# Local attention between two long convolutions: group norms on GpSimd, a flat count of background pieces, predicated first keys, earlier spectra

## The chip, the cores and the metric

The kernel runs on one NeuronCore of a Trainium2 chip. The metric is device time of one launch in microseconds (us), lower is better. The core's engines run side by side and meet through semaphores: TensorE (PE; its weight loads are listed as PEld), VectorE (DVE), ScalarE (ACT), GpSimd (POOL), and the queue on SyncE (SP) that issues most DMA transfers.

## The reference, cut to what matters

The data are `x` of 2048 tokens by 512 channels in bf16. Four residual layers follow each other, A, B, A, B:

```python
x = A_u
x = x + A(layernorm(x))   # long convolution per channel, by FFT, + u * Dskip
x = x + B(layernorm(x))   # local attention
x = x + A(layernorm(x))   # the same kernel spectra again
x = x + B(layernorm(x))   # the same weights again

def B(x):                 # 32 heads of 16; window 8, dilation 2
    q, k, v = split(x @ wqkv)                       # 512 -> 3 * 512
    idx = pos[:, None] - 2 * arange(8)[None, :]     # 8 keys behind each query, 2 apart
    attn = softmax(where(idx >= 0, q . k[idx] * 16 ** -0.5, -1e9))
    return (attn . v[idx]) @ wo
```

As the dilation is 2, even and odd tokens never meet: attention splits into two parities of 1024 tokens.

## The kernel before

**Stages.** Up to about 258 us the convolution kernels are built and the first convolution runs; the change leaves this part alone, but for the size of one statistics tile. `b_layer` is called twice (258 to 374 us and 438 to 557.5 us of the profiled span), `a_layer` once between them (374 to 438 us). In these functions the order of work on PE, DVE and ACT is the order in which it is written (`manual_schedule`); GpSimd and SP also take their instructions in program order, and an instruction that waits holds up what is queued behind it on its engine.

**`b_layer`, its steps.** The loop at the end runs 36 steps t = 0 to 35 (`N = 4 * NB`, `NB` = 9). A step handles 2 token blocks of one of four job sets n = t // 9. Set n has parity `n // 2` and one half of the heads (`n % 2`). A step consists of:

- `logits(t)`: 16 small products (L1098) into the one 4-bank PSUM tile S, then the exponential on ACT (L1101) that writes PT and so frees S;
- `work`: background pieces in the order of their due times. `proj` (L1056, two pieces of two matmuls 128x512) makes 512 tokens of one q or k feature group; DVE takes the result to a tile `st` (L1061), and SP sends even and odd features of it to `KS` or `QS` (L1072), where even and odd heads lie apart. `vproj` (L1081, one piece) makes V for one block, `out` (L1152, two pieces) the output projection of 128 tokens. All have PSUM tiles `psG`, of which there are three. The number of pieces of a step follows from the due times;
- `values(t - 2)`: 16 products of PT with V into the one PSUM tile O (L1117), then reciprocal and product on DVE (L1121, L1125);
- every third step `turn_o`: an SP transpose of the result (`oS`) and a GpSimd copy into `oT` (L1134);
- `late(t)`: the layer norm of token groups 2 and 3 (see below).

**`sets`** holds two pairs `KS`, `QS`, used by turns: logits(9) is the first step that reads those of n = 1. Their `proj` jobs run in steps 4 to 8.

**Groups.** The tokens are cut into four groups of four slots of 128; groups 0 and 1 are parity 0, groups 2 and 3 parity 1. Groups 0 and 1 are normed and transposed ahead of the loop. For groups 2 and 3 `late` does it in the loop: `gather` (bn_stats on DVE, L212), `aggregate` (DVE, L223, then a root on GpSimd, L225 and L226), `scales` (DVE, L230, L231), four `norm` calls (DVE, L260) into `xq`, two SP transposes into `xt` (L1216), and four GpSimd copies from `xt` into `XU` (L1220, its view here is `xnT`). The `proj` and `vproj` jobs of n = 2 and 3 read these columns; their earliest step is t = 13, that of the `out` jobs t = 24. For group 2, `late` gathers at t = 2 and 3, aggregates at 4, scales and norms at 6, and norms and transposes at 7; for group 3 all of it comes three steps later.

**First keys.** Ahead of the loop four `proj` jobs of n = 0 run: k = 0 and 2 (q and k of the first 512 tokens), then 1 and 3 (the next 512). Of k = 0 and 2, the first 240 columns (`FIRST`) go from PSUM to `QS` and `KS` by predicated copies on DVE (L1069), the others by ACT and SP DMAs. The loop starts behind all four.

**The tail.** The last steps emit `values` of two steps, `ahead` (dummy matmuls on L1284 and half an output piece), and `turn_last`, which transposes on PE in place of the DMA.

**`a_layer`** takes 16 chunks. For chunk k: `s1` (forward transform, evacuated into Z), `turns` (SP transposes of Z into zt, two chunks each) or `turn_pe`, `s2` (spectrum, L882, evacuated to `xc` on ACT, L886), `product` (DVE, L894, L895 and two more), `inverse` (into VT) and `final` (into X). At i = 14 and 15 it also gathers the statistics of groups 0 and 1 for the next layer, four slots of 384 columns at a time.

Of the kernel before, what the change touches and what calls it, by code (L numbers as in the profile page):

```python
# [11 lines left out]
ALU = mybir.AluOpType  # L12
# [87 lines left out]
def slot(m):  # L100

    g, i = m // 4, m % 4
    return 8 * (g % 2) + 2 * i + g // 2
# [93 lines left out]
class LnStats:  # L197
# [58 lines left out]
        nc.vector.scalar_tensor_tensor(self.nb[:, js], self.sums[:, 0, js], -1.0 / D, self.rstd[:, js], ALU.mult,  # L256
                                       ALU.mult)

    def norm(self, dst, src, j):
        self.nc.vector.tensor_scalar(dst, src, self.rstd[:, j:j + 1], self.nb[:, j:j + 1], ALU.mult, ALU.add)  # L260


def turn(nc, zt, Z, g0, n):
# [553 lines left out]
def a_layer(nc, tc, C, X, kt_dram, XU, ln_b, finish):  # L817

    with ExitStack() as es:
# [119 lines left out]
        with tc.manual_schedule(engines={mybir.EngineType.PE, mybir.EngineType.DVE, mybir.EngineType.Activation}):  # L939
            s1(0, on_dve)  # L940
            finish()
            s1(1, on_act)
            s1(2, on_dve)
            s1(3, on_act)
            zpair(0)
            warm(2)
            turn_pe(0)
            s1(4)
            s2(0, True)
            turns(2)  # L950
            turn_pe(1)
            s1(5, on_dve)
            for i in range(16):
                if i > 0:
                    s2(i)
                product(i)
                if i > 0:
                    inverse(i - 1, i > 10)
                if i + 6 < 16:
                    s1(i + 6)  # L960
                    if i % 4 == 1:
                        turns(i + 3)
                        turns(i + 5)
                if i >= 5:
                    final(i - 5, on_dve if i in (6, 8) else on_act)
                if i in (14, 15):
                    ln_b.gather(X, 0, (i - 14) * 4, (i - 14) * 4 + 4)
            final(11)
            inverse(15)
            for k in range(12, 16):  # L970
                final(k)


def b_layer(nc, tc, C, X, Wt, ln_b, XU, store=None, ln_next=None):

    with ExitStack() as es:
# [67 lines left out]
        st = {}  # L1044
        on_act, on_dve = nc.scalar.copy, nc.vector.tensor_copy

        def proj(n, k, eng=on_dve, early=False):

            par, fp = n // 2, n % 2
            f2, which, h = k // 4, k // 2 % 2, k % 2  # L1050
            if h == 0:
                st[n, which] = stp.tile([128, 1024], BF, name="st", tag="st")
            f0 = which * 512 + (fp * 2 + f2) * 128
            ps = gps([128, 512])
            for ct in range(4):
                nc.tensor.matmul(ps[:], wqk[:, ct, f0:f0 + 128], xnT[:, ct, par, UF + h * 512:UF + h * 512 + 512],  # L1056
                                 start=(ct == 0), stop=(ct == 3))
                if ct == 1:
                    yield
            if not early:  # L1060
                eng(st[n, which][:, h * 512:h * 512 + 512], ps[:])  # L1061
            else:
                eng(st[n, which][:, FIRST:512], ps[:, FIRST:512])
            if h or n == 0:
                T = sets[n % 2][1 - which]
                x0 = 0 if n else FIRST if early else 512 * h
                if early:
                    for e in range(2):
                        nc.vector.copy_predicated(T[:, e, f2, UF:UF + FIRST], par_rows[:, e:e + 1].to_broadcast([128, FIRST]),  # L1069
                                                  ps[:, 0:FIRST])  # L1070
# [35 lines left out]
        def values(t):  # L1106
            par, fp = t // NB // 2, t // NB % 2
            pt = PT[t % 3]
            for x in range(2):
                assert (par, fp, (t % NB * 2 + x) % NB) in ready, (t, x, done)  # L1110
            O = psO.tile([128, 16, DH + 1], F32, name="O", tag="O")
            for i in range(4):
                for sl in range(4):
                    x, e = sl // 2, sl % 2
# [74 lines left out]

        with tc.manual_schedule(engines={mybir.EngineType.PE, mybir.EngineType.DVE, mybir.EngineType.Activation}):  # L1190
            def warm(n):
                O = psO.tile([128, 16, DH + 1], F32, name="O", tag="O")
                for _ in range(n):
                    nc.tensor.matmul(O[:].rearrange("p a b -> p (a b)"), ident[:],
                                     C["F1"][:, 0:2].rearrange("p j r k -> p (j r k)")[:, 0:272], start=True, stop=True,
                                     skip_group_check=True)
            xq = {}

            def late(t):
                for g in (2, 3):  # L1200
                    u, m0 = t - 3 * g + 2, g * 4
                    if u in (-2, -1):
                        for p in range(len(ln_b.parts)):
                            ln_b.gather(X, p, m0 + 2 * u + 4, m0 + 2 * u + 6)
                    elif u == 0:
                        ln_b.aggregate(m0, m0 + 4, C["half"])
                    elif u == 2:
                        ln_b.scales(m0, m0 + 4)
                        xq[g] = ld.tile([128, 4, D], BF, name="xq", tag="xq")
                    if u in (2, 3):  # L1210
                        for i in (2 * u - 4, 2 * u - 3):
                            ln_b.norm(xq[g][:, i], X[:, slot(m0 + i), :], m0 + i)
                    if u == 3:
                        xt = ld.tile([128, 16, 128], BF, name="xt", tag="xt")
                        for h in range(2):
                            nc.sync.dma_start_transpose(xt[:, 8 * h:8 * h + 8],  # L1216
# [28 lines left out]
            fan(0, pt0, 1)  # L1245
            fan(1, pt1, 1)
            warm(6)
            for k in (0, 2):
                for _ in proj(0, k, on_act, True):
                    pass  # L1250
            for k, eng in ((1, on_act), (3, on_dve)):
                for _ in proj(0, k, eng):
                    pass
            psS = banks("b_psS", 1)
            jobs = []
            for n in range(4):
                p = n // 2
                for i, k in enumerate((4, 6, 5, 7) if n == 0 else range(8)):
                    k0 = i + 4 if n == 0 else i
                    jobs.append((NB * n - 1.5 + (k0 // 4 * 4 if n else 4 + i // 2 * 2), 2, proj(n, k), 0 if n < 2 else 13))  # L1260
                jobs += [(NB * n + b // 2 + 1 + b / 100, 1, vproj(p, n % 2, b), 0 if n < 2 else 13) for b in range(NB)]
            jobs += [(N - 9 + .8 * m, 2, out(m), 24) for m in range(8)]
            jobs.sort(key=lambda j: j[0])
# [21 lines left out]
                                     stop=True, skip_group_check=True)  # L1285
                omm(tail[m], m, (0, 1))
            for t in range(N):
                end = done + max(min(total - done, -(-(c - done) // max(1, int(d) - t + 1))) for d, c in due)
                logits(t)
                square()  # L1290
                work(end - 1, t)
                if 2 <= t < N - 1:
                    values(t - 2)
                work(end, t)
                if t >= N - 2:
                    assert not jobs
# [54 lines left out]
def kernel(  # L1351
# [70 lines left out]
```

## Time and profile before

| what | value |
|---|---|
| median of 5 runs (lowest, highest) | 558.1 us (557.04, 559.28) |
| the profiled execution: its own time, its span | 559.23 us, 557.5 us |
| granted TensorE clock, mean | 0.92 |
| busy time over the span: PE, DVE, ACT, POOL | 401.0, 434.1, 355.7, 72.9 us |
| layer B, first (258 to 374 us): PE, DVE, ACT, POOL busy | 101.81, 80.69, 84.62, 31.68 us |
| second convolution (374 to 438 us) | 52.67, 50.94, 47.48, 3.61 us |
| layer B, second (438 to 557.5 us) | 102.47, 77.98, 76.73, 18.27 us |

The span runs from the first to the last instruction of the profiled execution; 1.73 us of its time lie around it. A row of the page's groups gives a line, engine, operation and tile, busy time and mean duration, and the idle time just ahead of it with what ended that. A row of the timeline gives start, duration, engine, line, operation, output and inputs, and in brackets the idle time before it and its releaser. All times are of one execution.

### The profile page before, as it was taken

What the parts mean: (1) busy time and instruction counts of PE and PEld (TensorE: products, weight loads), DVE (VectorE), ACT (ScalarE), POOL (GpSimd) and SP (SyncE); (2) the same over time, 40 slices, a digit from 0 to 9 for tenths busy, and PEclk for the clock granted to TensorE, in tenths of its full rate; (3) what the DMA queues carried; (4) which work ended last, traced back from release to release, by engine and by line L of the source; (5) the groups of instructions that cost most, each with busy time, mean ns of one, the idle gap of its engine ahead of it and who ended that gap; (6) DMA issues with size and microseconds to landing.
All of it is one profiled execution on the core that took longest, in us unless ns stands there. A gap on an engine that the chain in (4) does not pass through costs nothing.

```text
span 557.5 us, 15293 instructions
## 1 busy us (share of the span) xinstructions
PE 401.0 (72%) x6530; PEld 255.9 (46%) x6530; DVE 434.1 (78%) x959; ACT 355.7 (64%) x439; POOL 72.9 (13%) x121
## 2 busy tenths in 40 slices
PE   1200665485668459698995999887898699599987
PEld 0100433354337136465553466555665455346654
DVE  5999998989979997676696576576897869657653
ACT  4999654364536346356766479865888676647762
POOL 0000000000000020543016111250000201611110
PEclk9999998698779778799998799997999999879999
DMA  8201057532463567334236132215782013513452
GB/s 275 111 1 38 2 113 98 86 125 59 95 115 115 116 73 207 65 125 155 93 92 124 54 105 60 39 45 146 165 167 48 2 49 95 121 54 105 100 74 77
DMA packets 100536, 52.79 MB, mean 95 GB/s; under 512 B 85363, under 2 KB 93428, under 8 KB 99188
## 3 DMA queue, kind: packets, MB, share of 16 engines
q1 hardware_dynamic: 97956, 48.01, 37.0%
q0 software_dynamic: 928, 3.41, 1.9%
q8 instruction: 51, 0.84, 0.7%
q10 hardware_dynamic: 1584, 0.39, 0.3%
q14 instruction: 17, 0.14, 0.1%
HBM read 17.96 MB, written 8.13 MB: 47 GB/s over the span
## 4 chain that ended last, share of the span: by engine, by line
PE 32%; DVE 28%; ACT 8%; DMA 6%; issue 4%; SPq 2%; POOL 1%; DVEq 0%; ACTq 0%; POOLq 0%
PE psG L1056 7%; DMA zt<-Z 4%; PE psG L1081 4%; PE O L1117 3%; ACT PT L1101 3%; PE S L1098 3%; DVE Ytab L656 3%; DVE ln_st_b L212 2%; DVE Y2tab L658 2%; PE psG L1152 2%; DVE ta L619 2%; DVE tb L620 2%; DVE st L1061 2%; DVE xq L260 2%; POOL XU L1220 1%
## 5 line engine op out<-in xcount | busy, mean ns | idle before, releaser
L1101 ACT ACTIVATE PT<-S 128x1824 bf16<-128x1824 f32 x72 | 121.7, 1690 | 55.3 <-PE S L1098 55.2
L1056 PE MATMUL psG<-XU,wqk 128*128 128x512 bf16 x256 | 71.8, 397 | 9.0 <-POOL XU L1220 8.3
L1061 DVE CAST st<-psG 128x512 bf16<-128x512 f32 x58 | 39.1, 680 | 27.2 <-PE psG L1056 26.9
L1117 PEld LDWEIGHTS <-PT 128*128 128x128 bf16 x1152 | 38.5, 97 | 21.7 <-DVE on L1125 10.3
L1117 PE MATMUL O<-V,PT 128*128 128x17 bf16 x1152 | 40.3, 171 | 8.1 <-DVE on L1125 7.9
L1081 PE MATMUL psG<-wv,XU 128*128 128x256 bf16 x288 | 39.5, 273 | 1.2 <-DVE st L1061 1.2
L307 PE MATMUL psA<-X,sb_F 128*128 128x128 bf16 x128 | 13.7, 242 | 36.4 <-ACT X L720 35.2
L307 PEld LDWEIGHTS <-sb_F 128*128 128x128 bf16 x256 | 16.9, 105 | 44.2 <-issue 41.8
L1121 DVE RECIPROCAL rd<-O 128x16 f32<-128x16 f32 x72 | 18.2, 253 | 22.7 <-PE O L1117 21.0
L1056 PEld LDWEIGHTS <-wqk 128*128 128x128 bf16 x256 | 21.0, 98 | 29.7 <-issue 14.5
L294 ACT CAST Z<-psA 128x1024 bf16<-128x1024 f32 (+1 forms) x32 | 28.8, 982 | 7.8 <-PE psA L307 7.8
L675 PE MATMUL psk<-Ytab,Xtab 128*32 128x64 bf16 x1024 | 24.2, 209 | 12.5 <-issue 6.5
L1125 DVE TENSOR_TENSOR on<-O,rd 128x256 bf16<-128x256 f32 x72 | 30.5, 424 | 2.5
L678 PE MATMUL psk<-Y2tab,Xtab 128*32 128x48 bf16 x1024 | 23.4, 206 | 12.1 <-issue 10.0
L1098 PEld LDWEIGHTS <-KS 32*128 32x128 bf16 x1152 | 19.0, 95 | 28.1 <-issue 25.4
L1098 PE MATMUL S<-QS,KS 32*128 32x114 bf16 x1152 | 28.6, 216 | 4.5 <-ACT PT L1101 2.7
L656 DVE TENSOR_TENSOR Ytab<-Ytab,MA 128x2048 bf16<-128x2048 bf16 (+1 forms) x33 | 30.6, 927 | 0.2
L658 DVE TENSOR_TENSOR Y2tab<-Ytab,MB 128x2048 bf16<-128x2048 bf16 (+1 forms) x33 | 30.5, 925 | 0.0
L684 ACT CAST KTq<-psk 128x1024 bf16<-128x1024 f32 (+1 forms) x9 | 8.3, 918 | 34.3 <-issue 28.9
L332 PE MATMUL psA<-zt,sb_C 128*128 128x512 bf16 x30 | 14.9, 524 | 20.7 <-DMA zt<-Z 20.7
L678 PEld LDWEIGHTS <-Xtab 128*32 128x32 bf16 x1024 | 21.2, 103 | 16.6 <-issue 15.7
L1081 PEld LDWEIGHTS <-XU 128*128 128x128 bf16 x288 | 24.9, 98 | 6.8 <-issue 1.3
(245 smaller groups left out, 1050.1 us busy)
## 6 DMA issues: line engine op xcount, KB each, us to landing
kt_scratch<-Kt SPq DMA_DIRECT2D x4, 1024.0 KB, 3.9
Kt<-kt_scratch SPq DMA_DIRECT2D x4, 1024.0 KB, 6.2
QS<-st SPq DMA_DIRECT2D x24, 128.0 KB, 2.0
KS<-st SPq DMA_DIRECT2D x24, 128.0 KB, 3.2
X<-in_A_u_dram SPq DMA_DIRECT2D x4, 512.0 KB, 5.2
out_dram<-X SPq DMA_DIRECT2D x16, 128.0 KB, 1.7
k_scratch<-KTq SPq DMA_DIRECT2D x7, 256.0 KB, 2.2
KT<-k_scratch SPq DMA_DIRECT2D x7, 256.0 KB, 2.9
```

The lines of the kernel that those rows point to most:

```text
L294: self.nc.scalar.copy(dst, src)
L307: nc.tensor.matmul(o, F1[:, j, r, :], rhs_j(j), start=True, stop=not dk)
L656: nc.vector.tensor_tensor(v(Y[:, :, :, q * EYB:(q + 1) * EYB, :]), src, vm(self.mult(self.MA, lev, hc, EYB)), ALU.mult)
L658: nc.vector.tensor_tensor(v(Y2[:, :, :, (q - 1) * EYB:q * EYB, :]), src, vm(self.mult(self.MB, lev, hc, EYB)), ALU.mult)
L678: nc.tensor.matmul(psk[32 * g:32 * g + 32, ds, EYB:], xs, Y2[:, 1 - m // 2, h, :, t], start=False, stop=(m == 3), skip_group_check=True)
L1056: nc.tensor.matmul(ps[:], wqk[:, ct, f0:f0 + 128], xnT[:, ct, par, UF + h * 512:UF + h * 512 + 512], start=(ct == 0), stop=(ct == 3))
L1061: eng(st[n, which][:, h * 512:h * 512 + 512], ps[:])
L1081: nc.tensor.matmul(ps[:].rearrange("p h d -> p (h d)"), xnT[:, ct, par, NQ * b + 1:NQ * b + 1 + NK], wv[:, ct, fp * 256:fp * 256 + 256], s ...
L1098: nc.tensor.matmul(S[:, i, sl * NQ:(sl + 1) * NQ], KS[r, e, f2, b * NQ + 1:b * NQ + 1 + NK], QS[r, e, f2, UF + b * NQ:UF + b * NQ + NQ], s ...
L1101: nc.scalar.activation(pt[:, 0:16 * NQ].rearrange("k (i x) -> k i x", i=4), S[:, :, 0:4 * NQ], ACT.Exp, scale=DH ** -0.5)
L1117: nc.tensor.matmul(O[:, x * 8 + i * 2 + e, :], pt[:, c0:c0 + 128], V[:, par * NB + b, (fp * 2 + f2) * 8 + i * 2 + e, :], start=True, stop= ...
L1125: nc.vector.tensor_tensor(on.rearrange("q (h d) -> q h d", d=DH), O[:, :, 0:DH], rd[:].unsqueeze(2).to_broadcast([128, 16, DH]), ALU.mult)
```

## The change

1. `norm` takes an engine, and `late` norms groups 2 and 3 on GpSimd: gathers at t = 0 and 1, aggregate at 2, scales, norms, transposes and copies all at 3; for group 3 two steps later.
2. The pieces of a step: four for t < 4 and from t = 28 on, three between, more only where the due times ask for it. Due times of the `proj` jobs are one step earlier, and those of n = 0 lie closer together.
3. `begun`, `placed` and `spread` stand for the first four `proj` jobs: q and k of the first 512 tokens go to `QS` and `KS` by predicated copies alone, in two parts of which the second stands behind logits(0); the product of k = 3 also comes behind logits(0) and uses the PSUM tile O.
4. At t = 33 to 35 the order of `values`, `ahead` and `turn_last` is another.
5. In `a_layer`, `s2` runs one chunk further ahead from i = 6 on, `s1(5)` stands behind the first product, the last finals stand behind the last inverses, and the gathers of groups 0 and 1 are spread over i = 10 to 15. For that, the statistics of layer 2 have three parts of 256, 128 and 128 columns in place of two of 384 and 128.

```diff
--- before.py
+++ after.py
@@ -256,8 +256,8 @@
         nc.vector.scalar_tensor_tensor(self.nb[:, js], self.sums[:, 0, js], -1.0 / D, self.rstd[:, js], ALU.mult,
                                        ALU.mult)
 
-    def norm(self, dst, src, j):
-        self.nc.vector.tensor_scalar(dst, src, self.rstd[:, j:j + 1], self.nb[:, j:j + 1], ALU.mult, ALU.add)
+    def norm(self, dst, src, j, eng=None):
+        (eng or self.nc.vector).tensor_scalar(dst, src, self.rstd[:, j:j + 1], self.nb[:, j:j + 1], ALU.mult, ALU.add)
 
 
 def turn(nc, zt, Z, g0, n):
@@ -949,13 +949,19 @@
             s2(0, True)
             turns(2)
             turn_pe(1)
-            s1(5, on_dve)
             for i in range(16):
-                if i > 0:
+                if 0 < i < 7:
                     s2(i)
+                if 6 <= i < 15:
+                    s2(i + 1)
                 product(i)
-                if i > 0:
+                if i == 15:
+                    inverse(14, True)
+                    inverse(15)
+                if 0 < i < 15:
                     inverse(i - 1, i > 10)
+                if i == 0:
+                    s1(5, on_dve)
                 if i + 6 < 16:
                     s1(i + 6)
                     if i % 4 == 1:
@@ -963,11 +969,11 @@
                         turns(i + 5)
                 if i >= 5:
                     final(i - 5, on_dve if i in (6, 8) else on_act)
-                if i in (14, 15):
-                    ln_b.gather(X, 0, (i - 14) * 4, (i - 14) * 4 + 4)
-            final(11)
-            inverse(15)
-            for k in range(12, 16):
+                if 10 <= i < 14:
+                    ln_b.gather(X, 0, 2 * i - 20, 2 * i - 18)
+                if i >= 14:
+                    ln_b.gather(X, 1, 4 * i - 56, 4 * i - 52)
+            for k in range(11, 16):
                 final(k)
 
 
@@ -1044,7 +1050,28 @@
         st = {}
         on_act, on_dve = nc.scalar.copy, nc.vector.tensor_copy
 
-        def proj(n, k, eng=on_dve, early=False):
+        def begun(k, pool=None):
+            f2, which, h = k // 4, k // 2 % 2, k % 2
+            f0 = which * 512 + f2 * 128
+            ps = pool.tile([128, 512], F32, name="O", tag="O") if pool else gps([128, 512])
+            for ct in range(4):
+                nc.tensor.matmul(ps[:], wqk[:, ct, f0:f0 + 128], xnT[:, ct, 0, UF + h * 512:UF + h * 512 + 512],
+                                 start=(ct == 0), stop=(ct == 3))
+            return ps
+
+        def placed(k, ps, a, b):
+            T = sets[0][1 - k // 2 % 2]
+            for e in range(2):
+                nc.vector.copy_predicated(T[:, e, k // 4, UF + a:UF + b], par_rows[:, e:e + 1].to_broadcast([128, b - a]),
+                                          ps[:, a:b])
+
+        def spread(k, ps, eng):
+            T, t = sets[0][1 - k // 2 % 2], stp.tile([128, 1024], BF, name="st", tag="st")
+            eng(t[:, 0:512], ps[:])
+            for e in range(2):
+                nc.sync.dma_start(T[e::2, e, k // 4, UF + 512:UF + 1024], t[e::2, 0:512])
+
+        def proj(n, k, eng=on_dve):
 
             par, fp = n // 2, n % 2
             f2, which, h = k // 4, k // 2 % 2, k % 2
@@ -1057,17 +1084,10 @@
                                  start=(ct == 0), stop=(ct == 3))
                 if ct == 1:
                     yield
-            if not early:
-                eng(st[n, which][:, h * 512:h * 512 + 512], ps[:])
-            else:
-                eng(st[n, which][:, FIRST:512], ps[:, FIRST:512])
+            eng(st[n, which][:, h * 512:h * 512 + 512], ps[:])
             if h or n == 0:
                 T = sets[n % 2][1 - which]
-                x0 = 0 if n else FIRST if early else 512 * h
-                if early:
-                    for e in range(2):
-                        nc.vector.copy_predicated(T[:, e, f2, UF:UF + FIRST], par_rows[:, e:e + 1].to_broadcast([128, FIRST]),
-                                                  ps[:, 0:FIRST])
+                x0 = 0 if n else 512 * h
                 for e in range(2):
                     nc.sync.dma_start(T[e::2, e, f2, UF + x0:UF + h * 512 + 512], st[n, which][e::2, x0:h * 512 + 512])
 
...
@@ -1189,28 +1209,26 @@
 
...
             xq = {}
 
             def late(t):
                 for g in (2, 3):
-                    u, m0 = t - 3 * g + 2, g * 4
-                    if u in (-2, -1):
+                    u, m0 = t - 2 * g + 4, g * 4
+                    if u in (0, 1):
                         for p in range(len(ln_b.parts)):
-                            ln_b.gather(X, p, m0 + 2 * u + 4, m0 + 2 * u + 6)
-                    elif u == 0:
+                            ln_b.gather(X, p, m0 + 2 * u, m0 + 2 * u + 2)
+                    elif u == 2:
                         ln_b.aggregate(m0, m0 + 4, C["half"])
-                    elif u == 2:
+                    elif u == 3:
                         ln_b.scales(m0, m0 + 4)
                         xq[g] = ld.tile([128, 4, D], BF, name="xq", tag="xq")
-                    if u in (2, 3):
-                        for i in (2 * u - 4, 2 * u - 3):
-                            ln_b.norm(xq[g][:, i], X[:, slot(m0 + i), :], m0 + i)
-                    if u == 3:
+                        for i in range(4):
+                            ln_b.norm(xq[g][:, i], X[:, slot(m0 + i), :], m0 + i, nc.gpsimd)
                         xt = ld.tile([128, 16, 128], BF, name="xt", tag="xt")
                         for h in range(2):
                             nc.sync.dma_start_transpose(xt[:, 8 * h:8 * h + 8],
@@ -1245,19 +1263,22 @@
             fan(0, pt0, 1)
             fan(1, pt1, 1)
             warm(6)
-            for k in (0, 2):
-                for _ in proj(0, k, on_act, True):
-                    pass
-            for k, eng in ((1, on_act), (3, on_dve)):
-                for _ in proj(0, k, eng):
-                    pass
+            half = [begun(0), begun(2), begun(1)]
+            for k in range(2):
+                placed(2 * k, half[k], 0, FIRST)
+            spread(1, half[2], on_act)
             psS = banks("b_psS", 1)
+            logits(0)
+            odd = begun(3, psO)
+            placed(0, half[0], FIRST, 512)
+            spread(3, odd, on_dve)
+            placed(2, half[1], FIRST, 512)
             jobs = []
             for n in range(4):
                 p = n // 2
                 for i, k in enumerate((4, 6, 5, 7) if n == 0 else range(8)):
                     k0 = i + 4 if n == 0 else i
-                    jobs.append((NB * n - 1.5 + (k0 // 4 * 4 if n else 4 + i // 2 * 2), 2, proj(n, k), 0 if n < 2 else 13))
+                    jobs.append((NB * n - 2.5 + (k0 // 4 * 4 if n else 4 + i // 2), 2, proj(n, k), 0 if n < 2 else 13))
                 jobs += [(NB * n + b // 2 + 1 + b / 100, 1, vproj(p, n % 2, b), 0 if n < 2 else 13) for b in range(NB)]
             jobs += [(N - 9 + .8 * m, 2, out(m), 24) for m in range(8)]
             jobs.sort(key=lambda j: j[0])
@@ -1285,18 +1306,25 @@
                                      stop=True, skip_group_check=True)
                 omm(tail[m], m, (0, 1))
             for t in range(N):
-                end = done + max(min(total - done, -(-(c - done) // max(1, int(d) - t + 1))) for d, c in due)
-                logits(t)
+                need = max([c for d, c in due if int(d) <= t] + [0])
+                end = min(total, max(need, done + (4 if t < 4 or t >= N - 8 else 3)))
+                if t:
+                    logits(t)
                 square()
                 work(end - 1, t)
                 if 2 <= t < N - 1:
                     values(t - 2)
                 work(end, t)
-                if t >= N - 2:
+                if t == N - 1:
                     assert not jobs
-                    values(t - 1)
-                    ahead(t - N + 10, 3)
-                if t >= N - 3:
+                    values(N - 3)
+                    ahead(8, 1)
+                    turn_last(N - 4)
+                    values(N - 2)
+                    ahead(9, 3)
+                elif t == N - 3:
+                    turn_last(t - 3)
+                elif t == N - 2:
                     turn_last(t - 3)
                 elif t >= 4 and t % 3 == 1:
                     turn_o(t // 3 - 1)
@@ -1382,7 +1410,7 @@
     X = kernel_and_first_conv(nc, tc, C, prm, A_u[0], const, kt_dram, kscr, ln, ln_b, W,
                                      B_wqkv.rearrange("(t p) f -> p t f", p=128)[:, :, 0:1024])
     const2 = ctx.enter_context(tc.tile_pool(reuse_waits="tile", name="const2", bufs=1))
-    ln_b2 = LnStats(nc, const2, [(0, 3 * DCH), (3 * DCH, D)], "b2", eps)
+    ln_b2 = LnStats(nc, const2, [(0, 2 * DCH), (2 * DCH, 3 * DCH), (3 * DCH, D)], "b2", eps)
     Wt = load_b_weights(nc, const2, W[:].rearrange("p a b c -> p a (b c)"), C, B_wqkv, B_wo)
     XU = Wt["XU"]
     finish = b_layer(nc, tc, C, X, Wt, ln_b, XU, ln_next=ln)
```

More of the change, by code (lines that the diff above doesn't have):

```diff
@@ L1110, in values @@
                 assert (par, fp, (t % NB * 2 + x) % NB) in ready, (t, x, done)
-            O = psO.tile([128, 16, DH + 1], F32, name="O", tag="O")
+            O = psO.tile([128, 512], F32, name="O", tag="O")[:, 0:16 * DH + 16].rearrange("p (a b) -> p a b", b=DH + 1)
             for i in range(4):
@@ L1191, in warm @@
             def warm(n):
-                O = psO.tile([128, 16, DH + 1], F32, name="O", tag="O")
+                O = psO.tile([128, 512], F32, name="O", tag="O")
                 for _ in range(n):
-                    nc.tensor.matmul(O[:].rearrange("p a b -> p (a b)"), ident[:],
+                    nc.tensor.matmul(O[:, 0:272], ident[:],
                                      C["F1"][:, 0:2].rearrange("p j r k -> p (j r k)")[:, 0:272], start=True, stop=True,
```

## The prediction

> **What bounds the kernel now.** I read the windows view for three stretches first: attention layer 1 (258 to 374 us), the second convolution (374 to 438), attention layer 2 (438 to 557.5). TensorE is busy for 101.8 of 116 us in layer 1, but no engine is full, so the order of time decides. Next the page's groups:
>
> ```profile
> L1101 ACT ACTIVATE PT<-S 128x1824 bf16<-128x1824 f32 x72 | 121.7, 1690 | 55.3 <-PE S L1098 55.2
> L1056 PE MATMUL psG<-XU,wqk 128*128 128x512 bf16 x256 | 71.8, 397 | 9.0 <-POOL XU L1220 8.3
> ```
>
> One exponential per step, 36 per layer. ScalarE waits for the logits, and TensorE waits 8.3 us for GpSimd's copies. The timeline of layer 1 shows where:
>
> ```profile
> 296.17 4.25 POOL L1220 COPY XU<-xt 128x512 bf16<-128x512 bf16 x4 [0.47 <-DMA xt<-xq]
> 296.21 2.26 DVE L260 TENSOR_SCALAR xq<-X,ln_rstd_b,ln_nb_b 128x512 bf16<-128x512 bf16 x2
> ...
> 299.68 1.22 DVE L260 TENSOR_SCALAR xq<-X,ln_rstd_b,ln_nb_b 128x512 bf16<-128x512 bf16 x2
> ...
> 301.18 1.26 SPq L1216 DMA_TRANSPOSE xt<-xq  x1
> ...
> 302.99 1.69 ACT L1101 ACTIVATE PT<-S 128x1824 bf16<-128x1824 f32 x1 [0.82 <-PE S L1098]
> 304.43 4.03 POOL L1220 COPY XU<-xt 128x512 bf16<-128x512 bf16 x4 [1.00 <-DMA xt<-xq]
> 305.53 0.58 PE L1056 MATMUL psG<-XU,wqk 128*128 128x512 bf16 x1 [2.65 <-POOL XU L1220]
> ...
> 308.51 1.44 PE L1056 MATMUL psG<-XU,wqk 128*128 128x512 bf16 x3 [0.41 <-POOL XU L1220]
> ...
> 311.85 1.69 ACT L1101 ACTIVATE PT<-S 128x1824 bf16<-128x1824 f32 x1 [7.17 <-PE S L1098]
> ...
> 319.92 1.69 ACT L1101 ACTIVATE PT<-S 128x1824 bf16<-128x1824 f32 x1 [0.86 <-PE S L1098]
> 322.47 1.69 ACT L1101 ACTIVATE PT<-S 128x1824 bf16<-128x1824 f32 x1 [0.86 <-PE S L1098]
> ...
> 327.28 1.69 ACT L1101 ACTIVATE PT<-S 128x1824 bf16<-128x1824 f32 x1 [0.54 <-PE S L1098]
> 329.51 1.69 ACT L1101 ACTIVATE PT<-S 128x1824 bf16<-128x1824 f32 x1 [0.54 <-PE S L1098]
> ```
>
> Three things are to be seen. At t=13 the projections of group 3 need XU; its last norm pair ends at 300.90, the copies run 304.43 to 308.46, and the exponential of t=14 comes 8.86 us after that of t=13 (9.39 in layer 2): a stall of about 6.3. Steps 15 to 18 with four pieces last 2.55 us and are TensorE's (logits .31, eight matmuls 1.83, values .41); three-piece steps last 2.23 to 2.28 and are the loop exponential, free PSUM, logits, exponential. Third, the copies.
>
> [...] a norm pair takes 2.26 us beside GpSimd's copies, 0.73 elsewhere. [...]
>
> ```profile
> L1161 POOL TENSOR_SCALAR XU<-X,ln_rstd_a,ln_nb_a x10: 767/767/769, 366.5 to 373.6; 128x512 bf16<-128x512 bf16 x10
> L1161 DVE TENSOR_SCALAR XU<-X,ln_rstd_a,ln_nb_a x5: 395/407/621, 373.9 to 376.9; 128x512 bf16<-128x512 bf16 x5
> ```
>
> 1.9 times VectorE's. [...] three matmuls took 1.44 us at 308.51, where two take .59 otherwise, and the step after the stall lasts 2.95.
>
> **The change, part by part.** Layer 1's times; negative is earlier.
>
> *Opening (t=0 to 3).* Only the first 240 columns of k0 and k2 (predicated copies, .36 each) stand before logits(0); k3 and the rest follow. logits(0) no longer waits for k1: exp(0) moves from 269.87 to about 268.4. But exp(1) waits for a V cast queued on ScalarE behind exp(0) and for the late predicated copies: 271.9 against 272.04. exp(2) waits for the KS transfer of k3 (issued about 270.5, landing 3.2): no gain. Four SP transfers fewer.
>
> *Norms of groups 2, 3.* Gathers (2 slots by 2 parts, 1.40 us), four of them, move from t=2,3,5,6 (as traced at 276.64, 279.79, 284.75, 288.99) to t=0 to 3. VectorE so carries 2.8 us more early, and 1.6 us of predicated copies, which delays evacuations: exp(3) to exp(6) come up to .4 late. From t=4 three pieces in place of four, .3 each, bring this back: exp(8) about 289.4 for 290.37.
>
> GpSimd's chain: scales of g2 end about 281.2; four norms of .767 to 284.3; transposes land, by the 3.5 us from norm to copy above, at 287.9; four copies of 1.05 to 292.1; an oT copy, .75, to 292.9; then only the four norms of g3, to 295.95, as they are queued behind g2's copies. SP issues their two transposes to 297.45. In the changed order the second KS transfer of job set n=1 stands behind these transposes on SP (before, ahead of them; in layer 2 both KS transfers do). Issued at 297.5, landing 2.0 to 3.3 (median 3.2, least 1.7): logits(9) about 300.1, **exp(9) 300.5 for 293.09, or 291.6 without this wait**. Everything on TensorE is queued behind logits(9).
>
> *What follows.* Group 3's copies end about 303.7, ahead of t=13 near 310: the stall there goes. The idle of some 9 us costs the clock, .9 as above. exp(14) = 300.5 + .9 + 5 x 2.24 = 312.6, **+.8**. The eight VectorE norms that leave (4.9 us) had only delayed casts inside steps with slack: nothing.
>
> *Pieces.* Before, t=13 to 18 have four, 19 to 32 three. After, 13 to 27 have three, 28 to 30 four, 31 six, 32 three. From exp(14) to exp(28): 33.42 before, 14 x 2.24 = 31.4, **-2.0**. From 28 to 34: 3 x .3 and six pieces against three 1.1, **+2.0**. If evacuation of three PSUM buffers limits the six-piece step, .5 more.
>
> *Tail.* exp(35) comes 4.71 after exp(34), values(35) 6.45 after: logits(35) stands behind values(33), three dummy matmuls and an output piece. It is now directly after logits(34)'s exponential; values(35) about 5.0 after: **-1.4**. Layer 1: .8 - 2.0 + 2.0 - 1.4 = **-.6**.
>
> *Second convolution.* Two gathers stand on VectorE's path:
>
> ```profile
> 430.60 1.93 DVE L212 BATCH_NORM_STATS2 ln_st_b<-X 128x6 f32<-128x384 bf16 x4
> 432.45 0.67 DVE L894 TENSOR_TENSOR pa<-xc,Kt 128x1024 bf16<-128x1024 bf16 x1
> 434.50 1.94 DVE L212 BATCH_NORM_STATS2 ln_st_b<-X 128x6 f32<-128x384 bf16 x4
> 436.35 0.68 DVE L913 CAST VT<-psV 128x512 bf16<-128x512 f32 x1
> ```
>
> After, they are spread over i=10 to 13 in VectorE's gaps, with a part of .85 at i=14: -1.9 -1.9 + .85 = -2.95. Spectra one chunk further ahead pull their waits for zt forward (s2(8) waits about 1.5 at i=7), then ScalarE, 2.7 us an iteration, sets the pace; s2(12) still waits to 420.8. I take 1.2 of the gain back: **-1.7** (from -3 to +.5).
>
> *Layer 2.* As layer 1, but three parts in each gather (+.26 a step, .8 in all) and both KS transfers behind the transposes (+.6): exp(14) **+1.5**; then -1.8, +2.0, -1.4: **+.3**.
>
> *Sum:* -.6 - 1.7 + .3 = **-2.0**. The profiled execution, 559.23 (span 557.5 and 1.73 around it), becomes 557.2; it is 1.1 above the median of 558.1, so the median becomes **556.1**.
>
> **Unknown costs.** No trace of before has GpSimd norms beside step work. Lowest .767 (L1161); highest 1.06, a L1220 copy beside casts. I take .767[...]. Eight norms on the chain: 0 to +2.4 per layer, since exp(9) moves one for one. The KS landing: 1.7 to 4.0, -.5 to +1.8. Waiting predicated copies at t=0: -.5 to +1.
>
> **The rivals.** *A, two stalls trade places* (my forecast): -2.0, give or take 3. *B, the queue order doesn't bind:* KS of n=1 lands by 293, as before; the t=9 stall is absent, exp(13) comes near 301, and only some 2.6 us are waited at t=13 for group 3's copies. Then each attention layer gains about 7: 558.1 - 14 - 1 = 543. For it: before, these transfers stood free of the transposes (xt at 298.51, KS at 286.80). Against it: SP takes its issues in order, and the order is fixed. *C, slower: GpSimd's chain is longer than I say.* At about 1 us a norm, or if SP stands between, the chain to logits(9) is 2.4 to 3 longer in both layers: +5, 558.1 - 2 + 5 = 561, up to 564 with the six-piece step's .5 and a colder clock. It decides from a norm of .95 us, or .75 us more anywhere on the chain, where -2.0 becomes an even result, and from 1.25 a slower one. For it: L1220's 1.06; against: the L1161 row's spread of 2 ns. *D, the change doesn't do what it says:* exp(0) early gains nothing, as exp(1) shows, and the convolution's ScalarE pace eats the gathers' gain: 558 to 559.
>
> **How the numbers follow.** Chances: A .47, B .12, C .35, D .06. A measurement of this kernel tells some 0.3%, 1.7 us, from no change. A alone (553 to 559) gives faster .26, same .18, slower .03; B is faster; C slower; D splits. Faster .40, same .20, slower .40. The range, 548 to 565, leaves out B's centre and C's far end, under .2.
>
> **What would show it.** Right: exp(9) follows exp(8) by 10 to 11 us, released through a KS transfer; no XU wait at t=13; norms on GpSimd near .77; 2.2 us steps from 14 to 27, 2.55 and over 3 at 28 to 31; no gather between the last products. Wrong: KS landed before the group 3 transposes were issued (B); norms of 1 us, or exp(14) over 314 (C).

## The result and the profile after

The changed kernel takes 559.61 us (median of 43 runs) against 557.07 (80 runs of the kernel before): ratio 1.0048, 95% interval 1.0035 to 1.0061. By the medians it is 2.5 us slower, by the interval 1.9 to 3.4. The forecast was 2.0 us faster; 559.6 lies inside its range, but on the other side of no change. The profiled execution took 560.21 us, span 558.4.

The two spans differ by only .9 us, but the part before attention layer 1 is another length in each execution: its first VectorE norm starts at 259.47 before and at 257.66 after, with the same instructions ahead of it. So all stages below are counted from that norm; from it to the end are 298.03 us before and 300.74 after, +2.71, which agrees with the medians. Line numbers of `b_layer` are up to 28 higher than before. Its groups on the page:

```profile
L1121 ACT ACTIVATE PT<-S 128x1824 bf16<-128x1824 f32 x72 | 121.7, 1690 | 52.5 <-PE S L1118 52.2
...
L1083 PE MATMUL psG<-XU,wqk 128*128 128x512 bf16 x224 | 63.9, 395 | 1.1 <-ACT V L1103 0.9
L1118 PE MATMUL S<-QS,KS 32*128 32x114 bf16 x1152 | 28.8, 214 | 24.4 <-DMA KS<-st 15.7
```

The 8.3 us for which projections waited on XU are gone. In their place the logits' row has 24.4 us of idle time, 15.7 of it for a KS transfer; before it had 4.5, most of it behind the exponential:

```profile
L1098 PE MATMUL S<-QS,KS 32*128 32x114 bf16 x1152 | 28.6, 216 | 4.5 <-ACT PT L1101 2.7
```

The timeline of layer 1 after:

```profile
285.41 4.12 POOL L1238 COPY XU<-xt 128x512 bf16<-128x512 bf16 x4 [1.95 <-DMA xt<-xq]
...
290.23 3.00 POOL L260 TENSOR_SCALAR xq<-X,ln_rstd_b,ln_nb_b 128x512 bf16<-128x512 bf16 x4
291.76 2.73 SPq L1234 DMA_TRANSPOSE xt<-xq  x2
294.54 0.58 SPq L1092 DMA_DIRECT2D KS<-st  x1
...
296.60 4.07 POOL L1238 COPY XU<-xt 128x512 bf16<-128x512 bf16 x4 [3.37 <-DMA xt<-xq]
297.00 0.48 PE L1118 MATMUL S<-QS,KS 32*128 32x114 bf16 x12 [7.20 <-DMA KS<-st]
...
297.58 1.69 ACT L1121 ACTIVATE PT<-S 128x1824 bf16<-128x1824 f32 x1 [8.79 <-PE S L1118]
...
307.79 1.69 ACT L1121 ACTIVATE PT<-S 128x1824 bf16<-128x1824 f32 x1 [0.37 <-PE S L1118]
310.01 1.69 ACT L1121 ACTIVATE PT<-S 128x1824 bf16<-128x1824 f32 x1 [0.54 <-PE S L1118]
```

Read down the chain: group 2's copies, then group 3's norms (at 290.23, their scales written by 283.86), then its two transposes on SP, and only then the last KS transfer that logits(9) needs. It is issued at 294.54, as the transposes end at 294.49; its data had been there since its twin, which sends the other half of the same `st` tile, was issued at 286.05. exp(9) (297.58) comes 10.48 us after exp(8); exp(14) (310.01) only 2.22 after exp(13). The stall of t=13 has become one of t=9, as forecast. The stages:

| from, to | before | after | difference | forecast |
|---|---|---|---|---|
| first norm of layer 1, exp(14) | 52.38 | 52.35 | -.03 | +.8 |
| exp(14), exp(28) | 33.42 | 31.89 | -1.53 | -2.0 |
| exp(28), exp(34) | 13.89 | 15.96 | +2.07 | +2.0 |
| exp(34), first transform of the convolution | 13.73 | 14.01 | +.28 | -1.4 |
| convolution, to the first norm of layer 2 | 67.72 | 68.46 | +.74 | -1.7 |
| first norm of layer 2, exp(14) | 52.26 | 53.10 | +.84 | +1.5 |
| exp(14), exp(28) | 33.22 | 31.23 | -1.99 | -1.8 |
| exp(28), exp(34) | 13.38 | 15.84 | +2.46 | +2.0 |
| exp(34), end | 18.03 | 17.90 | -.13 | -1.4 |
| sum | 298.03 | 300.74 | +2.71 | -2.0 |

Three rows carry the miss of 4.7: the two tails (2.95 together) and the convolution (2.44). The timeline of the first tail after:

```profile
359.59 0.57 PE L1118 MATMUL S<-QS,KS 32*128 32x114 bf16 x16 [1.28 <-ACT PT L1121]
...
360.09 0.60 PE L1137 MATMUL O<-V,PT 128*128 128x17 bf16 x16
360.27 1.69 ACT L1121 ACTIVATE PT<-S 128x1824 bf16<-128x1824 f32 x1
...
360.55 0.59 PE L1305 MATMUL psG<-sb_F,sb_ident 128*128 128x512 bf16 x1
...
360.93 1.06 PE L1172 MATMUL psG<-wo_t,oT 128*128 128x512 bf16 x2
...
362.45 1.44 PE L1305 MATMUL psG<-sb_F,sb_ident 128*128 128x512 bf16 x3
...
363.68 1.06 PE L1172 MATMUL psG<-wo_t,oT 128*128 128x512 bf16 x2
...
364.53 0.63 PE L1137 MATMUL O<-V,PT 128*128 128x17 bf16 x16
```

exp(35) now follows exp(34) by 2.41 us instead of 4.71, as forecast. But values(35) (364.53) come 6.67 after exp(34), not 5.0. Between them stand the values of two earlier steps, four dummy matmuls (whose results are overwritten) and four of the output pieces' matmuls. They run at half clock: the granted clock is .50 from 359.50 to 364.50, and three matmuls take 1.44 us. In the tail before, the row of three ahead of logits(35) was as slow, but the row behind it was not:

```profile
360.77 1.44 PE L1284 MATMUL psG<-sb_F,sb_ident 128*128 128x512 bf16 x3
...
364.10 0.81 PE L1284 MATMUL psG<-sb_F,sb_ident 128*128 128x512 bf16 x3
```

The timeline of the convolution after:

```profile
404.74 0.39 PE L881 MATMUL psB<-zt,sb_C 128*128 128x512 bf16 x1 [1.44 <-DMA zt<-Z]
...
405.60 0.38 PE L882 MATMUL psB<-zt,sb_C 128*128 128x512 bf16 x1 [0.47 <-DMA zt<-Z]
...
406.99 0.42 PE L908 MATMUL psV<-sb_IC,Y 128*128 128x256 bf16 x1
...
407.85 0.68 DVE L894 TENSOR_TENSOR pa<-xc,Kt 128x1024 bf16<-128x1024 bf16 x1
...
413.53 0.68 DVE L894 TENSOR_TENSOR pa<-xc,Kt 128x1024 bf16<-128x1024 bf16 x1
```

s2(8), now in iteration 7, waits 1.9 us for zt on TensorE, and the inverse behind it runs slower (.42 where the same row shows .27 at other times; the granted clock is .79 from 404.70 to 407.50 and .68 to 411.00). Product 9 follows product 8 by 5.68 us; before it was 3.21:

```profile
409.80 0.69 DVE L894 TENSOR_TENSOR pa<-xc,Kt 128x1024 bf16<-128x1024 bf16 x1 [0.30 <-ACT xc L886]
...
413.01 0.68 DVE L894 TENSOR_TENSOR pa<-xc,Kt 128x1024 bf16<-128x1024 bf16 x1
```

### The profile page after: what moved, and what is told of

Read it like the earlier page. It is cut to its first block, busy times and chain, and to the rows that moved or that the text cites. A ratio compares the mean times of both kernels' runs of the same rounds, so it can differ in the third digit from the quotient of the medians.

```text
span 558.4 us, 15290 instructions
## 1 busy us (share of the span) xinstructions
PE 399.3 (72%) x6526; PEld 257.4 (46%) x6526; DVE 429.2 (77%) x967; ACT 354.4 (63%) x435; POOL 85.1 (15%) x137
## 4 chain that ended last, share of the span: by engine, by line
PE 36%; DVE 22%; ACT 10%; DMA 5%; POOL 3%; issue 2%; SPq 2%; ACTq 0%; DVEq 0%; POOLq 0%
PE psG L1083 6%; ACT PT L1121 6%; DMA zt<-Z 5%; PE psG L1101 4%; PE S L1118 4%; PE O L1137 3%; PE psG L1172 3%; DVE Ytab L656 3%; DVE Y2tab L658 3%; DVE ln_st_b L212 2%; DVE ta L619 2%; DVE tb L620 2%; SPq L266 2%; POOL XU L1238 1%; POOL xq L260 1%
## 5 line engine op out<-in xcount | busy, mean ns | idle before, releaser
L1083 PE MATMUL psG<-XU,wqk 128*128 128x512 bf16 x224 | 63.9, 395 | 1.1 <-ACT V L1103 0.9
L1118 PE MATMUL S<-QS,KS 32*128 32x114 bf16 x1152 | 28.8, 214 | 24.4 <-DMA KS<-st 15.7
L1118 PEld LDWEIGHTS <-KS 32*128 32x128 bf16 x1152 | 20.3, 94 | 49.4 <-issue 38.0
L1154 POOL COPY oT<-oS 128x684 bf16<-128x684 bf16 x20 | 15.1, 757 | 101.3 <-DMA oS<-on 101.3
L633 POOL MEMSET Xtab<- 128x64 bf16 x8 | 1.6, 199 | 181.3 <-PE psk L678 153.3
```

The lines of the kernel that those rows point to most:

```text
L1118: nc.tensor.matmul(S[:, i, sl * NQ:(sl + 1) * NQ], KS[r, e, f2, b * NQ + 1:b * NQ + 1 + NK], QS[r, e, f2, UF + b * NQ:UF + b * NQ + NQ], s ...
```

## The experiments

Ratios are to the kernel before, measured beside each run, with 95% intervals; stage times are those of one profiled execution of each kernel, counted from the first norm of layer 1. Where the intervals of two kernels overlap, their medians alone don't settle which is faster.

**1. KS transfers ahead of the transposes.**

```diff
                         for i in range(4):
                             ln_b.norm(xq[g][:, i], X[:, slot(m0 + i), :], m0 + i, nc.gpsimd)
+                    if u == (3 if g == 2 else 6):
                         xt = ld.tile([128, 16, 128], BF, name="xt", tag="xt")
                         ...   # the transposes and copies, unchanged
```

> Edit of the kernel after: the transposes and XU copies of group 3 are emitted three steps later (t=8), so that both KS transfers of set n=1 stand ahead of them on SP; on GpSimd group 3's copies then stand behind one more oT copy. Theory (the wait at t=9 is only the queue's order): exp(9) follows exp(8) by about 2.5 us instead of 10.5; part of it comes back at t=13, as group 3's copies now end near 304 where logits(13) would be at 298: a wait of some 5 us for XU. Net 2.5 to 3.5 us less per attention layer, 559.6 - 6 = 553 to 555. Rival (GpSimd's longer chain is what costs, wherever it is met): the wait at t=13 takes the whole 8 us back, 559 to 560.

554.28 us, ratio .9964 (.9940 to .9989). In layer 1 exp(9) follows exp(8) by 3.42 us, and 4.30 lie between exp(13) and exp(14). The timeline of this kernel at t=13:

```profile
298.53 4.04 POOL L1239 COPY XU<-xt 128x512 bf16<-128x512 bf16 x4 [0.24 <-DMA xt<-xq]
...
302.62 0.59 PE L1083 MATMUL psG<-XU,wqk 128*128 128x512 bf16 x1 [0.41 <-POOL XU L1239]
...
305.10 1.69 ACT L1121 ACTIVATE PT<-S 128x1824 bf16<-128x1824 f32 x1 [2.61 <-PE S L1118]
```

Part of the gain comes back as a wait for XU, but exp(14) stays 4.9 us earlier than in the kernel after. In layer 2 one of group 3's transposes still stood ahead of KS, 9.31 us lie between exp(8) and exp(9), and exp(14) is only 1.9 us earlier. In layer 1, SP's order was the wait; the rival, which had the whole gain lost again at t=13, is out.

**2. Norms on VectorE, at the new steps.**

```diff
-                            ln_b.norm(xq[g][:, i], X[:, slot(m0 + i), :], m0 + i, nc.gpsimd)
+                            ln_b.norm(xq[g][:, i], X[:, slot(m0 + i), :], m0 + i)
```

> Edit of the kernel after: the eight norms of groups 2 and 3 of each layer run on VectorE again, at the steps they have now. The KS transfers of n=1 stay behind group 3's transposes (both of them, also in layer 1), and group 3's root stands behind group 2's copies on GpSimd. Theory (the queue's order costs, not GpSimd's norms): exp(9) moves by no more than 1.5 us, 557.5 to 559.6. Rival (the forecast's slower case, GpSimd's norms make the chain too long): 4 to 5 us less, near 555.

559.92 us, ratio 1.0055 (1.0034 to 1.0077), no better than the kernel after. exp(9) is .9 later, but exp(8) 8.5 later: the stall now begins at t=8. The timeline of this kernel:

```profile
284.01 4.08 POOL L1238 COPY XU<-xt 128x512 bf16<-128x512 bf16 x4 [6.95 <-DMA xt<-xq]
...
288.46 1.02 POOL L226 TENSOR_TENSOR ln_den_b<-ln_mv_b,half 128x4 bf16<-128x4 f32 x1
...
289.51 0.18 DVE L230 RECIPROCAL ln_rstd_b<-ln_den_b 128x4 f32<-128x4 bf16 x1 [5.26 <-POOL ln_den_b L226]
```

Group 3's root stands behind group 2's copies, and VectorE itself stands waiting for it, with its evacuations behind. In this order it makes no difference to the time which of the two engines does the norms.

**3. The old tail.** Edit: the branch for t=33 to 35 of the kernel before.

```diff
-                if t == N - 1:
-                    values(N - 3)
-                    ahead(8, 1)
...
+                if t >= N - 2:
+                    values(t - 1)
+                    ahead(t - N + 10, 3)
```

> Edit of the kernel after: steps t=33 to 35 as in the kernel before (values, ahead and turn_last in the old order); all else as after. Theory (the reorder only moved the same TensorE work from behind exp(34) to ahead of values(35), at half clock): from exp(34) to values(35) 6.4 us in both layers instead of 6.67 and 6.14; the time stays at 559.6 within 1 us. Rival (the forecast: the reorder gains 1.4 us per layer): 562.4.

558.22 us, ratio 1.0018 (1.0000 to 1.0037). exp(34) to the convolution 13.57 us, exp(34) to the end 18.71, together 32.28; after 31.91, before 31.76. But tails vary between executions: with the new order and its dummies the two together took 30.62 to 32.53 us in seven kernels, with the old order 31.76 to 32.95 in three. In the length of the tails a gain from the reorder is not shown; the rival's 562.4 is out.

**4. No dummy matmuls in the tail.**

```diff
-                    ahead(8, 1)
+                    ahead(8, 0)
...
-                    ahead(9, 3)
+                    ahead(9, 0)
```

> Edit of the kernel after: no dummy matmuls in the tail (ahead(8, 0) and ahead(9, 0) for ahead(8, 1) and ahead(9, 3)). Theory (the tail's step failed since dummy matmuls and output pieces at half clock stand ahead of values(35)): exp(34) to values(35) shrinks by 1 to 1.5 us from 6.67 in layer 1 and 6.14 in layer 2[...]; 557.5 to 559. Rival (values(35) is held by the chain of values(33), values(34) and their tile O): no change, 559.6.

558.14 us, ratio 1.0035 (1.0019 to 1.0051): 1.5 less than the kernel after, as the theory has it, but the intervals overlap. In the traces, values(35) come 5.25 and 5.04 us after exp(34) instead of 6.67 and 6.14, so the dummy matmuls stood on the path to them. The two tails take 12.90 and 16.88 us instead of 14.01 and 17.90, below all seven kernels with the dummies (from 13.07 and 17.55). In layer 1 half of this comes back, as the convolution takes .60 longer.

**5. s2 in its old place, in the kernel after.**

```diff
-                if 0 < i < 7:
-                    s2(i)
-                if 6 <= i < 15:
-                    s2(i + 1)
+                if i > 0:
+                    s2(i)
```

> Edit of the kernel after: in the second convolution s2(i) stands in iteration i again; the gathers stay spread and s1(5) stays behind the first product. Theory (the lead put the wait for zt(8) and its clock loss on TensorE's queue, which delayed s1, Z, and the transposes that s2(12) waits for): product(9) follows product(8) by some 3 us instead of 5.7, product(12) comes about 3 us earlier, and the stage ends about 3 us earlier: 556 to 557. Rival (the convolution is paced by ScalarE in either order, and the 5.7 us are a slow transfer of that one execution): 559.6 within 1 us.

555.82 us, ratio .9986 (.9970 to 1.0001). Product 9 follows product 8 by 3.20 us, product 12 is 4.7 us earlier, and the stage takes 64.69 us instead of 68.46. Of these 3.8 us, .9 are there at the first product already, ahead of the lead; why is open. From product 8 to the end of the stage, the six kernels with the lead take 31.90 to 32.73 us and the six with the new loop but without it 29.27 to 29.84: the lead costs some 2.7. The 3.84 to 5.77 us from product 8 to 9 show in all six with the lead, so they are no slow transfer of one execution.

Before, the stage took 67.72, 3.0 more than here. Only 1.2 of that lies behind product 8 (30.81 before, 29.61 here), where the old gathers stood. The larger part lies ahead: the first product comes 10.86 us after the first transform instead of 13.24. That fits the place of s1(5), now behind the first product, which no run tests alone.

**6. The convolution's other edits, in the kernel before.** Edit: the convolution's loop of run 5 (gathers spread, s1(5) behind the first product, finals behind the last inverses) and the statistics in three parts.

```diff
-                if i in (14, 15):
-                    ln_b.gather(X, 0, (i - 14) * 4, (i - 14) * 4 + 4)
+                if 10 <= i < 14:
+                    ln_b.gather(X, 0, 2 * i - 20, 2 * i - 18)
+                if i >= 14:
+                    ln_b.gather(X, 1, 4 * i - 56, 4 * i - 52)
```

> Edit of the kernel before: only the convolution's gathers (spread over i=10 to 15, statistics of layer 2 in three parts), s1(5) behind the first product, and finals behind the last inverses, s2 as before. Theory (this part of the change is good, and the lead of s2 lost it): the stage ends 3 to 4.5 us earlier; three-part gathers in layer 2 cost it less than 1: 557.1 - 3 = 553.5 to 554.5. Rival (the gain in the run with the old s2 was there only behind the other edits): 557 within 1 us.

555.80 us, ratio .9977 (.9953 to 1.0001). That lies between the theory's 553.5 to 554.5 and the rival's 556 to 558. In the trace the end comes 3.0 us earlier than before; the medians say 1.3, and their interval ends at no gain. The sign fits, the size is not settled. exp(14) of layer 2 comes 52.04 us after its first norm (before 52.26), so the three-part gathers cost nothing there.

**7. GpSimd and SP in a written order.** In both kernels the order of these two is laid by a scheduler, and not by the loop; here it is the order of the loop. Group 3's norms come ahead of group 2's copies, and its transposes behind the KS transfers (names shortened):

```diff
-        with tc.manual_schedule(engines={PE, DVE, Activation}):
+        with tc.manual_schedule(engines={PE, DVE, Activation, Pool, SP}):
...
+                for g in (2, 3):
+                    if t == {2: 3, 3: 7}[g]:   # transposes
+                    if t == {2: 5, 3: 7}[g]:   # copies, behind the norms of t=5
...
-                elif t >= 4 and t % 3 == 1:
+                elif t == 5 or t > 4 and t % 3 == 1:   # turn_o, now behind late(t)
```

> Edit of the kernel after: GpSimd and SP take their work in the order in which it is written; group 3's norms are written ahead of group 2's XU copies, group 3's transposes and copies at t=7 behind the KS transfers of n=1, and the first oS transpose and oT copy one step later. Theory (two orders, SP's at t=9 and GpSimd's behind it, are all of the wait): norms of group 3 end near 287, transposes land by 294, copies end by 298, so neither t=9 nor t=13 waits in either layer: exp(9) 2.5 us after exp(8), exp(13) to exp(14) 2.3. exp(28) 6.5 to 7.5 us earlier than after in each layer: 559.6 - 14 = 545 to 547. Rival (another transfer or the copies still bind, as in the run with KS ahead): 552 to 555.

540.07 us, ratio .9712 (.9676 to .9748). The timeline of this kernel:

```profile
285.60 3.01 POOL L260 TENSOR_SCALAR xq<-X,ln_rstd_b,ln_nb_b 128x512 bf16<-128x512 bf16 x4 [0.59 <-DVE ln_nb_b L231]
...
287.59 2.19 SPq L1092 DMA_DIRECT2D KS<-st  x2
...
288.56 4.11 POOL L1242 COPY XU<-xt 128x512 bf16<-128x512 bf16 x4
...
289.88 2.64 SPq L1237 DMA_TRANSPOSE xt<-xq  x2
...
291.86 1.69 ACT L1121 ACTIVATE PT<-S 128x1824 bf16<-128x1824 f32 x1 [1.52 <-PE S L1118]
...
294.61 4.16 POOL L1242 COPY XU<-xt 128x512 bf16<-128x512 bf16 x4 [1.25 <-DMA xt<-xq]
```

Norms first, then KS, then the transposes: exp(9) 3.22 us after exp(8), exp(14) 2.23 after exp(13), in layer 2 2.98 and 2.23. exp(28) is 8.45 us earlier in layer 1; in layer 2, counted from its own first norm, 9.40. Both stalls are gone, at once, and the theory's 545 to 547 was too cautious. Of the 19.5 us to the kernel after, run 1 gained 5.3 by moving group 3's transposes and copies later; what GpSimd's order gives without SP's was not run.

**8. Run 7 with s2 in its old place.** Edit: as run 5.

> The kernel with both orders, and s2(i) in iteration i again. Theory: the two edits touch different stages and add: 3.7 us less than the kernel with both orders alone, 541 to 543. Rival: the convolution's start moves against its transfers, and part of the 3.7 is lost: 544 to 547.

538.37 us, ratio .9670 (.9641 to .9698). The time lies below theory and rival, as run 7's did. By the medians the edit is worth 1.7 us and not 3.7, but the two intervals overlap. In the traces the convolution stage shrinks from 67.58 to 64.02 us, 3.6, as in run 5, so in that stage the two edits add; whether all of it reaches the end, six runs each don't settle.

**9. Run 8 without the dummy matmuls.** Edit: as run 4.

> The kernel with both orders and the old s2, without the dummy matmuls in the tail. Theory (the tail's dummies cost about 1 us in each layer, as the kernel after without them showed): 2 us less, near 536.5. Rival (with the earlier steps the tail waits for something else, GpSimd's norms or the oT copies): 538.4 within 1 us.

536.25 us, ratio .9643 (.9601 to .9685): 2.1 less than run 8, which fits the theory, but the intervals overlap. In the traces only the last tail keeps its gain, 1.2 us. In layer 1 the tail is 1.5 shorter and the convolution 1.5 longer, so from exp(34) to the first norm of layer 2 it is 77.84 us for 77.89; the theory's 1 us in each layer is not shown. This version beats both kernels, by some 20 us.

**10. Run 8 with the old rule for the pieces.**

```diff
-                need = max([c for d, c in due if int(d) <= t] + [0])
-                end = min(total, max(need, done + (4 if t < 4 or t >= N - 8 else 3)))
+                end = done + max(min(total - done, -(-(c - done) // max(1, int(d) - t + 1))) for d, c in due)
```

> The kernel with both orders and the old s2, with the old rule for the number of pieces of a step (the due times stay as in the kernel after). Theory (three pieces a step only move TensorE's work from t=14 to 27 to t=28 to 31, so the rule is worth nothing by itself): 538.4 within 1.5 us; steps after t=13 near 2.55 us, those of t=28 to 34 near 2.25. Rival (the flat count lets the exponential's loop run free and is worth 1.5 to 2 us a layer): 541.5 to 542.5.

542.68 us, ratio .9752 (.9711 to .9794), 4.3 us worse than run 8. The rival's size is right, but not its place: from exp(14) to exp(34) the old rule takes 47.16 us in layer 1 and the flat one 47.84. The loss of 2.9 us lies ahead of exp(14): steps of 2.55 us up to t=9, none of the pieces at t=11 and 12, and 4.34 us from exp(13) to exp(14) instead of 2.23, at a granted clock of .50 (299.60 to 304.20). In layer 2 it is 3.0 us.

**11. Run 9 with the old first keys.** Edit: `begun`, `placed` and `spread` replaced by the four `proj` calls ahead of the loop.

> The kernel with both orders, the old s2 and no dummies, with the first keys as in the kernel before (the first 240 columns by predicated copies, the rest by DMAs, logits(0) behind all four products). Theory (the opening brings exp(0) forward, but exp(1) takes it back, so it is worth little): exp(0) 1.5 us later in layer 1, exp(8) at most .5 later, 536.3 to 537.5. Rival (with the waits at t=9 and t=13 gone, exp(0)'s lead is kept, as exp(8) stands 1.5 us earlier in the kernel after): 1.5 us later in each layer, near 539.5.

537.67 us, ratio .9635 (.9588 to .9682): by the ratios no difference from run 9. In layer 1 exp(0) is 1.55 us later and exp(8) .21; the end, in the trace, comes within .03. The new first keys show no gain; the ratios would not show one of a microsecond or two.

## Why the prediction was wrong

- **The trade of two stalls (case A): right.** +7.4 was forecast for exp(9) and +6.3 measured; norms on GpSimd took .757 to .768 us for the .767 that was used. exp(14) came out at -.03 instead of +.8. The .9 for the clock, an estimate without its working, was 1.2 (exp(9) to exp(14): 12.43 us for 5 x 2.24): the granted clock was .50 from 294.50 to 300.00, as it had been at t=13 before, from 304.00 to 311.00.
- **The opening: right in the trace.** exp(0) came 1.55 us earlier (forecast 1.5), and in run 11 nothing of it is left at the end, as case D said of it.
- **The pieces: right as sizes, incomplete as a reason.** -1.53 and +2.07 stand against -2.0 and +2.0. That the flat count also relieves t=4 to 13 was hidden, as the wait at t=9 took it up; run 10 prices it at 2.9 and 3.0 us in the two layers, 4.3 net.
- **The tail, "-1.4" twice: wrong.** The failed step is "values(35) about 5.0 after". It asked when logits(35) would run, and not what still stands between them and values(35). Only two of six dummy matmuls were removed. values(33), one dummy and half an output piece moved from ahead of logits(35) to behind them, to the values(34), three dummies and half a piece that stood there already. Measured: 6.67 and 6.14 us, and +.28 and -.13 for the stages. Without dummies (runs 4, 9 and 11) it is 5.03 to 5.25: the forecast's number belongs to that kernel. The rest goes with the clock. In the fourteen tails with this code, values(35) come 6.42 to 6.72 us after exp(34) where the granted clock over 7 us from exp(34) is .52 to .60, and 5.79 to 6.14 where it is .76. The old order has 6.29 to 6.45 at .76: at the same clock the reorder gains some .4 there, not 1.4. The two profiles met different clocks, .76 in both layers before, .55 in layer 1 after.
- **The convolution, "1.2 of the gain back": wrong.** The lead of s2 costs some 2.7 us, 3.8 in the two traces of run 5, not 1.2. I had seen the wait of 1.5 and costed the wait alone. What is queued behind it on TensorE was not: the inverse at a lower clock (.79, then .68), s1, and so the next transposes, which were issued at 416.27 (158.61 from the first norm; before 154.98), 3.6 us later, so that s2(12) waited again (2.5 and .9 us; before .8). The gathers' -2.95 agrees with run 5's -3.0 by luck: only 1.2 of it came where the gathers stood, and the earlier first product, which gave the rest, has no term in the forecast.
- **Layer 2** was +1.18 instead of +.3. Its tail alone is 1.3 above the forecast, and the stages ahead of it .4 below. Its "+1.5" for exp(14) does not follow from the terms named, which make 2.2 (.8 as in layer 1, .8 and .6); .84 was measured, and run 6 shows nothing for the .8 of the three-part gathers.
- **The rivals.** C, a longer GpSimd chain, did not happen: no norm took 1 us. B's mechanism was not in this kernel, but its figure, 543, was about what the written order gives by other means (540.07).

Sum of the mis-sized terms: 2.95 for the tails and 2.44 for the convolution, less .7 elsewhere, make the 4.7 between -2.0 and +2.71.

## What to carry to other kernels

When work is started earlier, look at every queue that it passes: here norms and transposes moved ahead of a small transfer that more urgent work needed, and one order, of GpSimd and SP together, decided some 19 us. A reorder by itself removes nothing: list what stands ahead of the last dependent piece after it, with its clock. A wait that was pulled forward on TensorE here cost what was queued behind it, and once more where that fed the next wait. Before a part of a sum that came out right is called understood, see where in the stage its gain arose.

## What the runs showed of the hardware

- GpSimd's norms took the duration that they have elsewhere (.767 us in the kernel before) also where VectorE's casts and gathers ran beside them: group 2's four, from 279.06, took 3.01 us, and VectorE was busy for 2.97 of the 3.00 us from 279.00:

```profile
L260 POOL TENSOR_SCALAR xq<-X,ln_rstd_b,ln_nb_b x16: 757/765/768, 279.1 to 475.2; 128x512 bf16<-128x512 bf16 x16
```

- In the tail after, TensorE was busy for 2.03 of the 4.50 us from 355.00 to 359.50, with no gap over 1.28, and the granted clock was .50 for the next 5.00.
- The stage before layer 1, with the same work in all kernels here, took from 255.06 to 259.47 us in thirteen profiles. exp(0), counted from its end, comes at 8.85 or 8.86 in all ten kernels that have the new first keys, and at 10.40 in the three others. So part of the spread between executions lies there; why is open. The tails, at seven kernels with the same code, spread by 1.0 and 1.1 us.
